# Landmark transposes on both partition halves, and batch 1's loads by halves among the weights, in a fused attention and MLP kernel

## The chip, the cores and the metric

The kernel runs on one core of one Trainium2 chip. The metric is device time in microseconds (us), lower is better. Five engines work on their own instruction queues and meet at semaphores: TensorE (PE in the profile, PEld for its weight loads), VectorE (DVE), ScalarE (ACT), GpSimd (POOL) and SyncE (SP). PE writes to PSUM; DVE and ACT take its results from there into the on-chip memory SBUF. POOL and SP issue transfers to the DMA engines: here POOL issues all loads but the first small one, with a cast from float32 to bfloat16, and SP issues the stores and the transposing transfers.

## The reference

There are 8 batches of 8 heads, 576 tokens and a head width of 64. Each head has 32 landmark rows `p`. The landmarks attend to the tokens, and the tokens then attend to the packed landmarks. The result goes through a two-layer network with a smooth ReLU between (the reference calls its arguments moe, but there is one expert).

```python
def sm_attn(qq, kk, vv):
    s = scale * np.matmul(qq, kk.transpose(0, 1, 3, 2))
    a = np.exp(s - np.max(s, axis=-1, keepdims=True))
    a = a / (np.sum(a, axis=-1, keepdims=True) + 1e-09)
    return np.matmul(a, vv)
p_packed = sm_attn(p, k, v)
x = sm_attn(q, p_packed, p_packed)       # then tokens x 512
h = x @ w_in                             # 512 -> 2048
g = np.where(h >= 1, h, np.where(h <= -1, 0.0, (h + 1) ** 2 / 4))
return g @ w_out                         # 2048 -> 512, 4608 rows
```

## The kernel before

**The work of one batch.** `attention(b, key)` makes these steps, and the letters are the ones that the planner and the profile use. `kT` and `qT`: k and q are transposed by PE for batches 0 to 2 (tile `tp`, L382, copied to SBUF at L325) and by transposing DMAs that SP issues for batches 3 to 7 (L525). Each has two parts of four heads. `sc`: scores of the landmarks (`sp`, L403) and their exponential on ACT (`ex`, L406). `pk`: packed landmarks and their sums (L423, L429), then three small steps on DVE and ACT to `ppT` (L325, L439) and `rs` (L442). `s2`: scores of the tokens (`s`, L457) and `eT` (L462). `sm`: the sums over landmarks (L467), `ln` and `rc` on ACT (L471, L475) and the normalised weights `A` on DVE (L485). `M`: the packed landmarks times one quarter of `w_in` (`mp`, L506), cast to bfloat16 (L325); there are four, `M0` to `M3`, one for each part of `w_in`.

**The network.** `hidden_tile(b, fi)` makes one of 16 tiles of 128 hidden units for the 576 tokens of a batch: four matmuls `h` (L561), one ACT step (L566), one on ACT or DVE (L573 or L571), one DVE step that writes `hT` (L576). `out_tile(pr, i)` makes one of the 9 tiles of 128 output rows of a pair of batches: 16 matmuls `o` of 512 columns (L619), one for each part of `hT`, accumulated in one of two PSUM tiles that are kept for this (`psO`, NO = 2), then a copy to `ob` and the stores by SP (L634). Output tiles 0 to 3 of a pair need batch `2 pr` alone; tiles 4 to 8 need the second batch too.

**Split output tiles.** The parts of `w_out` arrive late at the start. For the first pair, the first `PARTS` output tiles are therefore cut at step `CUT`: the sum up to there is copied out of PSUM to `part` (`kept`, L622), which frees the PSUM tile, and is added when the rest is done (L630). Before, four tiles are cut at step 12, that is, ahead of the last part of `w_out`.

**Landmark transposes.** `add_pT(b0, b1, ...)` (L329) transposes the landmarks of batches b0 to b1 - 1 into `pT`. For each batch one 128x128 transpose on PE (L337) turns two column blocks c (heads 0 to 3, and 4 to 7) at once. `pT` wants head h on the upper or lower 64 partitions according to x, and both are filled, so four copies for (c, x) move 64 partitions each from `tpp` (L343). It is called for batches 0 and 1 at the start, and for batches 2 to 7 after one load `p` (L317) with key 0.9.

**Loads.** The first six are halves of k, v and q of batch 0 (`FIRST`). Then `ORDER` gives the order of the four parts of `w_in` (i0 to i3), the four of `w_out` (o0 to o3), and k, v and q of batch 1; a digit after k, v or q means four of the heads, a bare letter means all eight. Then come `p` and, for each later batch, k, q and v. All go through POOL's one queue, in this order.

**The planner.** Nothing of the order on the chip is decided by the hardware: `Plan.run` places each task on an engine (PE, ACT, DVE, SP, or the DMA queue) at the earliest time by its own clock, using the costs in the table `C`; among tasks that could start at about the same time it prefers the lower key. It writes the instructions of each engine in that order, and at run time each engine keeps to it and waits at semaphores. `C["half"]`, `C["part"]`, `C["w_in"]` and so on are its DMA costs, `C["land"]` the time from the end of a transfer in its model to its landing, `C["xt"]` and `C["xland"]` cost and landing of a transposing DMA. [...] `PB = 2` is the number of batches in the first landmark load. In `psW` there are three large PSUM tiles (NW) for everything but `o`.

Of the kernel before, what the change touches and what calls it, by code (L numbers as in the profile page):

```python
# [8 lines left out]

C = dict(load=3.5666, half=1.46, w_in=2.57, w_out=2.57, rest=1.25, out=9, p=4.05, land=2.0125, xt=6.5, xland=11,
         tpp=0.06, tp=0.042, sc=0.034, pk=0.9765, s2=0.2862, sm=0.245, M=0.2415, h=0.49, o=0.217, switch=0.05,
         join=0.1604, pTc=0.1, Tca=1.12, Tcd=0.76, ex=0.82, ppT=0.42, ppo=0.41, ppa=0.4, ppd=0.2, rs=0.18, eT=0.74,
         ln=0.65, rc=0.68, A=0.82, Mca=1, Mcd=1.22, x=0.65, ta=0.683, td=0.489, hT=0.758, oba=0.585, obd=0.6276,
         array=0.2, wake=1.2, warm=4.2, early=0.3, tell=0.034, feed=0.085, slack=0.51, margin=0.1717, wait=0.5,
         klo=0.05, khi=0.05, part=1.7833)
NW, NO, NX, NB = 3, 2, 5, 6
DW, FILL = 256, 512
PARTS, CUT = 4, 12  # L20

ORDER = "i0 i1 o0 i2 o1 i3 o2 k0 k1 v q0 q1 o3"
TURNED = 3


# [11 lines left out]
class Plan:  # L37
# [152 lines left out]
def kernel(  # L190
# [10 lines left out]
    nc = tc.nc  # L201
    f32 = mybir.dt.float32
    bf16 = mybir.dt.bfloat16
# [18 lines left out]
    X = 2  # L222
# [55 lines left out]
    hT = hid.tile([P, KF, 2 * S], bf16)  # L278
# [5 lines left out]
    L = {}  # L284
# [24 lines left out]
    for nm in ORDER.split():  # L309
# [4 lines left out]
        else:  # L314
            i = int(nm[1])
            L[nm[0], 1, i] = add(DMA, C["part"], -1, (), lambda nm=nm, i=i: load(nm[0], 1, HS[i]))
    L["p"] = add(DMA, C["rest"], -1, (), lambda: nc.gpsimd.dma_start(p_nat[:, PB * 2:], p_v[:, PB * 2:]))  # L317


    def both(fns, cost_a, cost_d, key, deps, **kw):  # L320

        return add((DVE, ACT), {ACT: cost_a, DVE: cost_d}, key, deps, fns, **kw)

    def copy(out_, in_):
        return lambda eng: nc.vector.tensor_copy(out_, in_) if eng == DVE else nc.scalar.copy(out_, in_)  # L325
# [3 lines left out]
    def add_pT(b0, b1, key, deps, cast):  # L329
        n, box = b1 - b0, {}  # L330

        def mm():
            if cast:
                nc.vector.tensor_copy(p_nat[:, 2 * b0:2 * b1], p_raw)
            tp = box["tp"] = wide([P, 8, H // 2, NP], bf16, "tpp")
            for b in range(b0, b1):
                nc.tensor.transpose(tp[:, b - b0].rearrange("p h n -> p (h n)"),  # L337
                                    p_nat[:, 2 * b:2 * b + 2].rearrange("p c d -> p (c d)"), ident)
        t = add(PE, C["tpp"] * n, key, deps, mm, takes="W", readers=4)
        res = []  # L340
# [339 lines left out]
    for b in range(B):  # L680
        if b + 2 < B:
            add_load("k", b + 2, deps=K[b, "kt"])
            add_load("q", b + 2, deps=K[b, "qt"])
            add_load("v", b + 2, deps=K[b, "pk"])
        K[b, "h"] = [hidden_tile(b, fi, b + fi / KF) for fi in range(KF)]
        if b == 0:
            attention(1, keys[1])
            add_pT(PB, B, 0.9, [L["p"]], False)
        if b % 2 == 1:
            for i in range(NT):  # L690
                out_tile(b // 2, i)
        if 0 < b < B - 1:
            attention(b + 1, keys[b + 1])
# [34 lines left out]
```

## Time and profile before

| | us |
|---|---|
| runs of the kernel before: median (lowest to highest of 3) | 248.82 (248.51 to 250.06) |
| the profiled execution: its own time | 249.7 |
| the span in its profile, first to last instruction | 247.8 |
| granted TensorE clock, mean | 1.000 |
| DVE busy | 181.9 (73%), 315 instructions |
| ACT busy | 185.6 (75%), 293 instructions |
| POOL busy | 29.1 (12%), 44 instructions |

All times in the views count from the first instruction of the span. A row of the view of groups gives line, engine, operation, what is written from what, shapes, count, busy time, mean ns of one, and the idle time of the engine just before. In the chain of waits each row has start, duration and what ran. In the table by stretches each engine has its busy time and, in brackets, its instructions; behind them stand the granted clock, the share of the DMA engines in use and the GB/s moved. A DMA row gives the KB and the us from its issue to its landing.

### The profile page before, as it was taken

The page shows a single profiled execution, that of the slowest core. Times are in us where ns is not written, and L with a number is a line of the kernel's source. Part 1 is how long each engine was busy: PE and PEld are TensorE (multiplying, and loading weights), DVE is VectorE, ACT ScalarE, POOL GpSimd, SP SyncE. Part 2 cuts the span into 40 slices and gives each one's busy share as a digit, 9 for nine tenths or more (in the row PEclk, how much of TensorE's full clock was granted, in tenths as well). Part 3 has the DMA queues.
Part 4 walks back from the last instruction along what each step waited for, and adds up shares of the span by engine and source line. Part 5 has one row for each costly group of instructions (what it writes and reads, how often), then busy time and mean ns, then how long its engine had stood idle before and what let it go on. Part 6 is the DMA issues. An engine that isn't in the chain of part 4 may idle for free.

```text
span 247.8 us, 5367 instructions
## 1 busy us (share of the span) xinstructions
PE 235.8 (95%) x2156; PEld 137.5 (55%) x2191; DVE 181.9 (73%) x315; ACT 185.6 (75%) x293; POOL 29.1 (12%) x44
## 2 busy tenths in 40 slices
PE   7979799999989999999999999999999999999994
PEld 2645476367626754666456644665466545654443
DVE  5356988889997988698859884699579976994000
ACT  3259796799899998698769888698888886993110
POOL 8632241211001030011101100000000000000000
PEclk9999999999999999999999999999999999999999
DMA  6999999999999999969796994641662031112222
GB/s 95 194 206 207 206 203 196 202 221 257 169 191 161 218 208 222 209 84 177 158 144 144 170 192 98 131 85 32 115 67 68 7 80 42 46 31 76 64 85 85
DMA packets 54761, 34.37 MB, mean 139 GB/s; under 512 B 27472, under 2 KB 50256, under 8 KB 54736
## 3 DMA queue, kind: packets, MB, share of 16 engines
q0 software_dynamic: 24672, 18.55, 50.3%
q1 hardware_dynamic: 29920, 15.41, 31.4%
q8 instruction: 17, 0.28, 0.5%
q14 instruction: 8, 0.07, 0.1%
q10 hardware_dynamic: 144, 0.07, 0.1%
HBM read 37.22 MB, written 9.44 MB: 188 GB/s over the span
## 4 chain that ended last, share of the span: by engine, by line
PE 76%; DMA 11%; DVE 6%; ACT 3%; issue 2%; POOL 1%; ACTq 0%; POOLq 0%
PE o L619 45%; PE h L561 20%; DMA w_in_sb<-in_moe_w_in_dram 8%; DVE hT L576 3%; DMA k<-in_k_dram 3%; PE mp L506 3%; PE pk L423 2%; PE sp L403 2%; PE tp L382 1%; DVE x L571 1%; PE sm L467 1%; PE s L457 1%; PE pk L429 1%; DVE ob L630 1%; ACT rc L475 1%
## 5 line engine op out<-in xcount | busy, mean ns | idle before, releaser
L619 PE MATMUL o<-w_out_sb,hT 128*128 128x512 bf16 (+2 forms) x559 | 136.0, 373 | 2.4 <-issue 0.8
L576 DVE SCALAR_TENSOR_TENSOR hT<-x 128x576 bf16<-128x576 f32 x128 | 94.6, 755 | 5.1 <-ACT x L573 2.1
L566 ACT ACTIVATE x<-h 128x576 f32<-128x576 f32 x128 | 78.0, 657 | 13.1 <-PE h L561 10.3
L619 PEld LDWEIGHTS <-hT 128*128 128x128 bf16 x592 | 55.2, 98 | 56.3 <-issue 5.8
L561 PE MATMUL h<-A,M 128*128 128x288 bf16 x512 | 75.1, 286 | 1.3 <-ACT M L325 0.5
L561 PEld LDWEIGHTS <-M 128*128 128x128 bf16 x512 | 49.5, 98 | 21.5 <-issue 1.1
L571 DVE TENSOR_SCALAR x<-x 128x576 f32<-128x576 f32 x87 | 39.8, 457 | 11.0 <-ACT x L566 11.0
L573 ACT ACTIVATE x<-x 128x576 f32<-128x576 f32 x41 | 27.2, 682 | 0.1
L325 DVE COPY ob<-o 128x512 f32<-128x512 f32 (+1 forms) x15 | 10.2, 677 | 20.5 <-DMA out_dram<-ob 17.2
L325 ACT COPY ob<-o 128x512 f32<-128x512 f32 (+1 forms) x18 | 10.2, 568 | 19.5 <-PE o L619 19.3
L325 ACT CAST M<-mp 128x1024 bf16<-128x1024 f32 x22 | 21.3, 1019 | 3.7 <-PE mp L506 3.7
L406 ACT ACTIVATE ex<-sp 96x768 bf16<-96x768 f32 x16 | 13.0, 814 | 5.4 <-PE sp L403 5.4
L325 DVE CAST M<-mp 128x1024 bf16<-128x1024 f32 x10 | 12.1, 1220 | 6.2 <-PE mp L506 6.2
L485 DVE SCALAR_TENSOR_TENSOR A<-eT,rs,rc 128x576 bf16<-128x576 bf16 x14 | 11.4, 813 | 5.1 <-ACT rc L475 5.1
L462 ACT ACTIVATE eT<-s,rs 128x576 bf16<-128x576 f32 x16 | 11.3, 739 | 4.7 <-PE s L457 4.7
L268 POOL DMA_DIRECT2D q<-in_q_dram x10 | 7.3, 733 | 49.7 <-DMA qT<-q 34.8
L471 ACT ACTIVATE ln<-sm 128x576 f32<-128x576 f32 x16 | 10.4, 651 | 3.6 <-PE sm L467 3.2
L506 PE MATMUL mp<-w_in_sb,ppT 64*32 64x512 bf16 x256 | 10.5, 380 | 2.6 <-DMA w_in_sb<-in_moe_w_in_dram 2.4
L697 PE MATMUL o<-zeros 128*128 128x512 bf16 (+1 forms) x37 | 11.5, 442 | 1.5 <-DVE zeros L256 1.2
L268 POOL DMA_DIRECT2D k<-in_k_dram x10 | 7.5, 748 | 41.2 <-DMA kT<-k 25.6
L475 ACT ACTIVATE rc<-ln 128x576 f32<-128x576 f32 x16 | 10.9, 683 | 0.5
L403 PEld LDWEIGHTS <-kT 128*128 128x128 bf16 x192 | 7.6, 98 | 2.8 <-DVE kT L325 0.9
(51 smaller groups left out, 120.0 us busy)
## 6 DMA issues: line engine op xcount, KB each, us to landing
out_dram<-ob SPq DMA_DIRECT2D x23, 192.0 KB, 2.3
v<-in_v_dram POOLq DMA_DIRECT2D x7, 576.0 KB, 18.3
k<-in_k_dram POOLq DMA_DIRECT2D x6, 576.0 KB, 12.6
q<-in_q_dram POOLq DMA_DIRECT2D x6, 576.0 KB, 11.8
out_dram<-ob SPq DMA_DIRECT2D x22, 128.0 KB, 3.4
w_in_sb<-in_moe_w_in_dram POOLq DMA_DIRECT2D x4, 512.0 KB, 14.7
w_out_sb<-in_moe_w_out_dram POOLq DMA_DIRECT2D x4, 512.0 KB, 16.8
out_dram<-ob SPq DMA_DIRECT2D x22, 64.0 KB, 2.0
```

The lines of the kernel that those rows point to most:

```text
L268: nc.gpsimd.dma_start(tok[nm, b][:, hs].rearrange("p h c d -> p h (c d)"), SRC[nm][b, hs].rearrange("h (p c) d -> p h (c d)", c=NC))
L325: return lambda eng: nc.vector.tensor_copy(out_, in_) if eng == DVE else nc.scalar.copy(out_, in_)
L403: nc.tensor.matmul(o[:, :, a], kT()[:, i, w:w + P], pT[:, b, h], start=True, stop=True)
L406: nc.scalar.activation(ex()[:, :, i].rearrange("p e x a n -> p e (x a n)"), box["sp"], AF.Exp, scale=scale)
L475: nc.scalar.activation(box["rc"], box["ln"], AF.Exp, scale=-1.0)
L506: nc.tensor.matmul(mp[a * NP:(a + 1) * NP, g], pp_of(y, h), w_in_sb[y * D:(y + 1) * D, h // 2, f * FW:(f + 1) * FW], start=True, stop=True)
L561: nc.tensor.matmul(h[:, hf, :HALF], T[b, "M"][:, g, fi * P:(fi + 1) * P], T[b, "A"][:, g, hf], start=(g == 0), stop=(g == G - 1))
L566: nc.scalar.activation(box["x"], box["h"][:, :, :HALF], AF.Prelu, bias=-1.0, alpha=0.5)
L571: nc.vector.tensor_scalar(x, x, 1.0, 0.0, ALU.add, ALU.max)
L573: nc.scalar.activation(x, x, AF.Relu, bias=1.0)
L576: nc.vector.scalar_tensor_tensor(hT[:, fi, col:col + S].rearrange("p (a t) -> p a t", a=2), box["x"], 1.0, box["x"], ALU.min, ALU.mult)
L619: nc.tensor.matmul(box["o", j][:, :cs.stop - cs.start], hT[:, fi, i * P:(i + 1) * P], w_out_sb[:, fi, cs], start=(fi == 0 or fi in cuts), ...
```

## The change

- `ORDER` is changed from `i0 i1 o0 i2 o1 i3 o2 k0 k1 v q0 q1 o3` to `i0 i1 o0 i2 o1 k0 v0 k1 i3 v1 o2 q1 q0 o3`. Batch 1's v comes in halves, and with it the packing step `pk` of batch 1 is made in two parts of four heads (L538 of the kernel before already chooses so).
- One output tile is cut instead of four, at step 8 instead of 12.
- The landmark transposes write each 64-column block straight to both halves of the partitions: four transposes of 128x64 for a batch instead of one of 128x128, and two copies (for x) of all eight heads instead of four copies of four heads.
- The second landmark load and its transposes are split: batches 2 and 3 (load after o3, key 0.9) and batches 4 to 7 (load after k, q and v of batch 2, key 1.9).
- Many of the planner's costs, the keys of the first attention steps and their order are changed.

```diff
-C = dict(load=3.5666, half=1.46, w_in=2.57, w_out=2.57, rest=1.25, out=9, p=4.05, land=2.0125, xt=6.5, xland=11,
-         tpp=0.06, tp=0.042, sc=0.034, pk=0.9765, s2=0.2862, sm=0.245, M=0.2415, h=0.49, o=0.217, switch=0.05,
...
-         array=0.2, wake=1.2, warm=4.2, early=0.3, tell=0.034, feed=0.085, slack=0.51, margin=0.1717, wait=0.5,
-         klo=0.05, khi=0.05, part=1.7833)
+C = dict(load=3.7557, half=1.46, w_in=2.57, w_out=2.57, rest=1.25, out=5.8085, p=4.05, land=2.9041, xt=4.025,
+         xland=23.0908, tpp=0.06, tp=0.042, sc=0.035, pk=1.0185, s2=0.2115, sm=0.245, M=0.4562, h=0.49, o=0.2105,
...
+         oba=0.5674, obd=0.661, array=0.2, wake=1.2, warm=4.2, early=0.3, tell=0.0394, feed=0.1, slack=0.7935,
+         margin=0.1545, wait=0.465, klo=0.0612, khi=0.0367, part=1.46, p4=1.9)
-PARTS, CUT = 4, 12
+PARTS, CUT = 1, 8
-ORDER = "i0 i1 o0 i2 o1 i3 o2 k0 k1 v q0 q1 o3"
+ORDER = "i0 i1 o0 i2 o1 k0 v0 k1 i3 v1 o2 q1 q0 o3"
-    L["p"] = add(DMA, C["rest"], -1, (), lambda: nc.gpsimd.dma_start(p_nat[:, PB * 2:], p_v[:, PB * 2:]))
+    def add_p(b0, b1):
+        L["p", b0] = add(DMA, C["rest"] * (b1 - b0) / 6, -1, (), lambda: nc.gpsimd.dma_start(p_nat[:, 2 * b0:2 * b1], p_v[:, 2 * b0:2 * b1]))
+    add_p(PB, 4)
-            tp = box["tp"] = wide([P, 8, H // 2, NP], bf16, "tpp")
+            tp = box["tp"] = wide([P, 4, H, NP], bf16, "tpp")
             for b in range(b0, b1):
-                nc.tensor.transpose(tp[:, b - b0].rearrange("p h n -> p (h n)"),
-                                    p_nat[:, 2 * b:2 * b + 2].rearrange("p c d -> p (c d)"), ident)
-        t = add(PE, C["tpp"] * n, key, deps, mm, takes="W", readers=4)
-        for c in range(2):
-            for x in range(X):
-                res.append(both(lambda eng, c=c, x=x: copy(pT[x * D:(x + 1) * D, b0:b1, 4 * c:4 * c + 4, x],
-                                                           box["tp"][c * D:(c + 1) * D, :n])(eng),
-                                C["pTc"] * n, C["pTc"] * n, key, [t], frees=t))
+                for c in range(2):
+                    for x in range(X):
+                        nc.tensor.transpose(tp[x * D:(x + 1) * D, b - b0, 4 * c:4 * c + 4].rearrange("p h n -> p (h n)"),
+                                            p_nat[:, 2 * b + c], ident)
+        t = add(PE, C["tpp"] * n * 2, key, deps, mm, takes="W", readers=X)
+        cost = 0.1 + 0.165 * n
+        res = [both(lambda eng, x=x: copy(pT[x * D:(x + 1) * D, b0:b1, :, x], box["tp"][x * D:(x + 1) * D, :n])(eng),
+                    cost * 1.3, cost, key, [t], frees=t) for x in range(X)]
-    names = "kT0 sc0 pk0 qT0 s20 kT1 sc1 pk1 sm0 qT1 s21 M0 sm1 M1 M2 M3".split()
+    names = "sc0 kT1 pk0 kT0 pk1 sc1 s20 qT0 qT1 M0 s21 sm1 M1 sm0 M2 M3".split()
-    order = "kT0 kT1 sc0 qT0 sc1 qT1 pk0 pk1 s20 M0 s21 sm0 M1 sm1 M2 M3".split()
+    order = "kT0 sc0 kT1 qT0 sc1 qT1 pk0 s20 M0 pk1 sm0 s21 sm1 M1 M2 M3".split()
-            add_pT(PB, B, 0.9, [L["p"]], False)
+            add_pT(PB, 4, 0.9, [L["p", PB]], False)
+            add_p(4, B)
+            add_pT(4, B, C["p4"], [L["p", 4]], False)
```

More of the change, by code (lines that the diff above doesn't have):

```diff
@@ L8 @@
 from concourse._compat import with_exitstack
-C = dict(load=3.5666, half=1.46, w_in=2.57, w_out=2.57, rest=1.25, out=9, p=4.05, land=2.0125, xt=6.5, xland=11,
-         tpp=0.06, tp=0.042, sc=0.034, pk=0.9765, s2=0.2862, sm=0.245, M=0.2415, h=0.49, o=0.217, switch=0.05,
-         join=0.1604, pTc=0.1, Tca=1.12, Tcd=0.76, ex=0.82, ppT=0.42, ppo=0.41, ppa=0.4, ppd=0.2, rs=0.18, eT=0.74,
-         ln=0.65, rc=0.68, A=0.82, Mca=1, Mcd=1.22, x=0.65, ta=0.683, td=0.489, hT=0.758, oba=0.585, obd=0.6276,
-         array=0.2, wake=1.2, warm=4.2, early=0.3, tell=0.034, feed=0.085, slack=0.51, margin=0.1717, wait=0.5,
-         klo=0.05, khi=0.05, part=1.7833)
+C = dict(load=3.7557, half=1.46, w_in=2.57, w_out=2.57, rest=1.25, out=5.8085, p=4.05, land=2.9041, xt=4.025,
+         xland=23.0908, tpp=0.06, tp=0.042, sc=0.035, pk=1.0185, s2=0.2115, sm=0.245, M=0.4562, h=0.49, o=0.2105,
+         switch=0.0658, join=0.1024, pTc=0.1, Tca=1.12, Tcd=0.7372, ex=0.82, ppT=0.42, ppo=0.41, ppa=0.4, ppd=0.2,
+         rs=0.18, eT=0.74, ln=0.65, rc=0.68, A=0.8193, Mca=1, Mcd=1.22, x=0.65, ta=0.683, td=0.457, hT=0.758,
+         oba=0.5674, obd=0.661, array=0.2, wake=1.2, warm=4.2, early=0.3, tell=0.0394, feed=0.1, slack=0.7935,
+         margin=0.1545, wait=0.465, klo=0.0612, khi=0.0367, part=1.46, p4=1.9)
 NW, NO, NX, NB = 3, 2, 5, 6
 DW, FILL = 256, 512
-PARTS, CUT = 4, 12
-ORDER = "i0 i1 o0 i2 o1 i3 o2 k0 k1 v q0 q1 o3"
+PARTS, CUT = 1, 8
+ORDER = "i0 i1 o0 i2 o1 k0 v0 k1 i3 v1 o2 q1 q0 o3"
 TURNED = 3
@@ L334, in mm @@
                 nc.vector.tensor_copy(p_nat[:, 2 * b0:2 * b1], p_raw)
-            tp = box["tp"] = wide([P, 8, H // 2, NP], bf16, "tpp")
+            tp = box["tp"] = wide([P, 4, H, NP], bf16, "tpp")
             for b in range(b0, b1):
-                nc.tensor.transpose(tp[:, b - b0].rearrange("p h n -> p (h n)"),
-                                    p_nat[:, 2 * b:2 * b + 2].rearrange("p c d -> p (c d)"), ident)
-        t = add(PE, C["tpp"] * n, key, deps, mm, takes="W", readers=4)
-        res = []
-        for c in range(2):
-            for x in range(X):
-                res.append(both(lambda eng, c=c, x=x: copy(pT[x * D:(x + 1) * D, b0:b1, 4 * c:4 * c + 4, x],
-                                                           box["tp"][c * D:(c + 1) * D, :n])(eng),
-                                C["pTc"] * n, C["pTc"] * n, key, [t], frees=t))
+                for c in range(2):
[6 more added lines that the diff above has]
+                    cost * 1.3, cost, key, [t], frees=t) for x in range(X)]
         for b in range(b0, b1):
```

## The prediction

> **What bounds the kernel now.** I read the page first (busy shares, the chain's shares), then the table by stretches, then the chain and the timeline around the stretches in which PE is not full.
>
> ```profile
> span 247.8 us, 5367 instructions
> ...
> PE 235.8 (95%) x2156; PEld 137.5 (55%) x2191; DVE 181.9 (73%) x315; ACT 185.6 (75%) x293; POOL 29.1 (12%) x44
> ...
> PE 76%; DMA 11%; DVE 6%; ACT 3%; issue 2%; POOL 1%; ACTq 0%; POOLq 0%
> ```
>
> PE is the bound over the whole span, so the time is PE's work plus what PE loses. DMA's 11% is the start, where loads set the pace. DVE and ACT have 9% together, and it lies in one place, as the stretches show:
>
> ```profile
> 40.00:44.00 4.00, 3.94 (x84) 2.79 (x83) 3.05 (x7) 1.43 (x4) 0.12 (x1) 1.00 1.60 191
> 44.00:48.00 4.00, 3.84 (x53) 1.54 (x47) 3.77 (x5) 3.31 (x5) 1.41 (x2) 1.00 1.35 204
> 48.00:52.00 4.00, 3.47 (x31) 2.11 (x31) 2.71 (x5) 3.83 (x7) 0.00 (x0) 1.00 1.28 224
> 68.00:72.00 4.00, 3.70 (x38) 1.41 (x37) 3.75 (x7) 4.00 (x7) 0.00 (x0) 1.00 1.28 191
> 72.00:76.00 4.00, 3.39 (x37) 1.16 (x36) 3.96 (x7) 3.37 (x6) 0.00 (x0) 1.00 1.28 191
> 88.00:92.00 4.00, 4.00 (x25) 2.15 (x22) 3.32 (x7) 3.98 (x7) 1.50 (x3) 1.00 1.32 176
> ```
>
> The last row is how it goes from 76 us on: PE full. In 40 to 44 ACT works 1.43 of 4 us: batch 0's hidden tiles are done, and batch 1's attention waits for its loads. In 48 to 52 and 68 to 76 PE idles again (0.5, 0.3, 0.6). The chain says for what:
>
> ```profile
> 48.76 0.91 ACT M L325
> 49.71 0.65 PE h L561 x4
> ...
> 73.38 0.39 PE o L619
> ```
>
> Batch 1's first hidden tile starts at 49.71, released by an ACT step. From there to 73.38 the chain runs mostly through DVE and ACT (its 6% and 3% of the page). So two things are for sale before 76 us: when batch 1's hidden tiles start (I call it the gate), and how much work DVE and ACT have after it.
>
> **The change part by part. The loads.** Two single rows each give an issue and its time to landing:
>
> ```profile
> 24.97 0.67 POOL L268 DMA_DIRECT2D q<-in_q_dram  x1 [1.86 <-DMA w_in_sb<-in_moe_w_in_dram]
> 27.55 0.75 POOL L296 DMA_DIRECT2D w_out_sb<-in_moe_w_out_dram  x1 [1.91 <-DMA w_out_sb<-in_moe_w_out_dram]
> ```
> ```profile
> q<-in_q_dram POOLq DMA_DIRECT2D x1, 288.0 KB, 16.2
> ```
> ```profile
> w_out_sb<-in_moe_w_out_dram POOLq DMA_DIRECT2D x1, 512.0 KB, 16.4
> ```
> ```profile
> 11.51 18.82 DMA w_in_sb<-in_moe_w_in_dram
> ```
>
> The last half of q lands at 24.97 + 16.2 = 41.2, o3 at 27.55 + 16.4 = 44.0, i3 at 11.51 + 18.82 = 30.3. The queue moves about 204 GB/s (the row of 44 to 48), so a half of 288 KB takes 1.44 us and a weight part of 512 KB 2.56. The same bytes stand ahead of the last half of q and ahead of o3 in both orders, so both land when they did. Three halves now precede i3: it lands at 30.3 + 4.3 = 34.6, k's first half at about 29.2, v's second at 36.1, o2 at 38.6. The gap that i3's delay opens for batch 0's last four hidden tiles is filled by batch 1's kT, sc and pk, which used to make the thin stretch at 40 to 44. By 38 us the packed landmarks of batch 1 are done, and so M's matmuls and casts no longer compete with the last steps.
>
> **The gate.** After q's last half these steps are in series, and their rows of now are:
>
> ```profile
> 42.90 0.68 PE L382 MATMUL tp<-ident,q 96*128 96x96 bf16 x12
> ...
> 43.62 0.76 DVE L325 COPY qT<-tp 128x1152 bf16<-128x1152 bf16 x1 [0.47 <-PE tp L382]
> ...
> 45.11 0.74 ACT L462 ACTIVATE eT<-s,rs 128x576 bf16<-128x576 f32 x1 [0.48 <-PE s L457]
> ...
> 46.66 0.41 PE L467 MATMUL sm<-eT,onesblk 128*128 128x288 bf16 x2
> ...
> 48.80 0.82 DVE L485 SCALAR_TENSOR_TENSOR A<-eT,rs,rc 128x576 bf16<-128x576 bf16 x1 [0.52 <-ACT rc L475]
> ...
> 49.53 0.68 DVE L325 COPY part<-o 128x512 f32<-128x512 f32 x1
> ```
>
> The transpose starts 1.7 us after the landing, `sm` 0.8 us after `eT` ends (45.85), and 1.7 us lie between `sm`'s end (47.07) and `A`, in which `ln` and `rc` ran on ACT behind those of the other four heads. In series without the first two delays: 0.68 + 0.76 + 0.4 (an estimate for `s` and its hop, 45.11 less the end of the copy at 44.38 being 0.73) + 0.74 + 0.41 + 1.7 + 0.82 = 5.5. From 41.2 that is 46.7 against 49.7: a gain between 0.1 (only the M cast leaves; `A` ends at 49.62 as now) and 3.0. I take 1.9, two thirds, because what stood in front of these steps (pk, both q transposes together, the M casts) is mostly done by then. What is late next is q's landing itself.
>
> **DVE and ACT after the gate.** The landmark copies of now, by size:
>
> ```profile
> L325 DVE COPY pT<-tpp 64x768 bf16<-64x768 bf16 x3 | 1.7, 551 | 0.9 <-ACT pT L325 0.9
> ...
> L325 DVE COPY pT<-tpp 64x256 bf16<-64x256 bf16 x2 | 0.6, 290 | 1.3 <-ACT pT L325 1.3
> ```
>
> Four copies of 768 elements cost at least 4 x 0.55 = 2.2, all on DVE. Between these rows a DVE copy grows by 0.51 ns an element, so one of 512 is 0.42 and one of 1024 is 0.68: two and two make 2.2 as well. The pair for batches 2 and 3 (0.84) may fall ahead of the gate, though. Of the copies of cut tiles three go, and the last of them stands at 49.53 (0.68), behind the gate; the adds become plain copies, which I take to be as long. So 0.7 to 1.5 of work leaves two engines, 0.35 to 0.75 of time; I take 0.6. With the gate, batch 2's hidden tiles start 2.5 us earlier. `pk` of batch 1 in two parts adds some three small DVE or ACT steps ahead of 40 us, in the thin stretch: nothing, as long as it stays thin; about 0.3 otherwise.
>
> **PE's own account.** That gain stays only if PE has done the same work by then:
>
> ```profile
> L619 PEld LDWEIGHTS <-hT x41: 95/98/99, 23.6 to 44.0; 128*128 128x128 bf16 x41
> ```
> ```profile
> L619 PEld LDWEIGHTS <-hT x52: 95/98/99, 23.6 to 48.6; 128*128 128x128 bf16 x52
> ```
> ```profile
> 220.56 10.74 PE o L619 x49
> ```
> ```profile
> L506 PEld LDWEIGHTS <-ppT 64*32 64x32 bf16 x256 | 3.1, 90 | 7.6 <-DMA w_in_sb<-in_moe_w_in_dram 4.0 <-issue 3.0
> ```
>
> By o3's landing 41 `o` steps had been issued, and by the gate 52, at 10.74/49 = 0.219 each in a run. With one cut tile at 8 and two PSUM tiles, at most 8 + 12 + 12 = 32 steps can be done before o3. Between 44.0 and the new gate at 47.8 some 13 more fit beside `s` and `sm`: 45, so 7 are owed (1.5 us). Transposes: 24 for batches 2 to 7 instead of 6. At 128 columns each, a quarter of an `o` step, 0.054, that is 18 x 0.054 = 1.0 more; their loads count 0.1 each if nothing hid them (the nearest rows, 90 ns for a narrow one), 24 x 0.1 - 0.3 = 2.1. I take 1.0. [...]
>
> Against these 2.5 us stands PE's idle time from 44 to 52 and 68 to 76: 0.16 + 0.53 + 0.30 + 0.61 = 1.6, and a lone `o` matmul is booked at 0.39 where it costs 0.219, so some 2.0. Net -0.5.
>
> **Edits at nothing.** The first landmarks: eight small transposes and two copies ahead of 7 us wait for nothing that is late, since k's transposed copy is what the first scores wait for; at worst they add 0.3 to a start that later loads absorb. The load for batches 4 to 7 moves behind k, q and v of batch 2, which land 1.3 us (256 KB) earlier for it; it is needed by scores half a span later. The planner's costs run nowhere on the chip, they change order and the number of filler matmuls: 0, with -0.9 to +0.9. The cost and landing of transposing DMAs move SP's queue and batches 3 to 7's scores, in a region where PE is full and neither kT nor qT releases the chain.
>
> **The sum.** 1.9 + 0.6 - 0.5 = 2.0 us less. The profiled execution (249.7, its span 247.8 and 1.9 around it) would become 247.7. It lies 0.9 above the median of the runs, so on the median's scale 248.8 - 2.0 = 246.8.
>
> **The rivals.** *Larger gain (0.21).* The order falls out as the loads allow: gate 3.0, DVE and ACT 0.75, PE's debt fully hidden in its idle time: 3.75, so 245.1 (244.3 to 245.8). For it speaks that PE's waits for `w_in` (4.0 in the L506 row) may shorten too, since the planner's landing time grows by 0.9 and they show PE ahead of the loads. Against it, that every step of the gate would have to meet an idle engine.
>
> *No change that counts (0.22).* The gate moves by 1 us or less, because A of the second group stays behind other ACT work, or PE's debt is not hidden: 247.8 to 249.5.
>
> *Slower (0.18).* Place: the two PSUM tiles for `o`. From o1's landing on both are held by tiles that cannot end before o3, so PE starves until 44 us. If the planner lets tile 0's rest hold one of them, 24 steps are done instead of 41: 17 x 0.219 = 3.7. If PE finds no idle time later, that and 1.0 of transposes stand against 1.9 + 0.6, or less of those where hidden tiles queue behind `o`: 248.8 + 4.7 - 2.5 = 251.0, to 252.5. It decides where fewer than some 92 steps are done when batch 2's hidden tiles start.
>
> *A start-up cost for each transfer (0.03).* Were a transfer not prepared behind the one before it, the split of v would push q's last half and o3 back. The rows bound this: o3 lands 2.8 after q's last half where its bytes take 2.56, so 0.24 by them, and a half's own time again, 1.44, at the other end. With 1.44 the gate gains 0.5, and the time is 248.2. [...]
>
> **How the numbers follow.** The forecast (gain 1.0 to 3.0, 245.8 to 247.8) has 0.36, and about a third of it lies under 246.3. Runs here tell 1% (2.5 us) from no change. Faster by more: 0.21 + 0.12 = 0.33. Slower by more, above 251.3: most of its rival, 0.14. Within: 0.53. The range from 244.9 to 250.6 leaves out about a tenth on either side.
>
> **What would show it.** Right: first `h` of batch 1 at 47 to 48.5 with q's last half landed at 41 and o3 at 44; ACT in 40 to 44 above 2.5 of 4; fewer than 35 hT loads before 44 but 98 or more by batch 2's first `h`, at 73 to 75; PE idle under 1 us in the four stretches from 44 to 52 and 68 to 76. Wrong: the gate at 49 or later; q landing after 42.5; transposes above 0.08 each; PE idle between 30 and 44 above 4 us; or a new wait behind 76 us, where I expect the rest to be shifted as it is.

## The result, and the profile after

| | before | after |
|---|---|---|
| median of the runs, us (lowest to highest of 20 each) | 249.38 (248.51 to 250.06) | 249.69 (249.25 to 250.32) |
| the profiled execution, us | 249.7 | 249.65 |
| its span, us | 247.8 | 247.6 |

The ratio is 1.0016, with a 95% interval of 1.0008 to 1.0023: the change costs 0.3 us by the medians (0.2 to 0.6 by the interval), where a gain of 2.0 was forecast. The median of before over 20 runs lies 0.56 above that of the three runs that the forecast started from, so its 246.8 would stand at 247.4 on this scale. The single profiled executions differ by 0.05 in their own time and by 0.2 in their spans, the other way, so the views below can place microseconds, not the last half of one. Some executions got a granted clock of 0.991 to 0.993 and took one to four us longer; five of the twelve runs of e2 and four of the twelve of e9 below are of this kind, and their other runs have medians of 249.59 and 249.28, within 0.15 of before's in the same rounds.

The page of the kernel after, span, engines and the chain's shares by engine:

```profile
span 247.6 us, 5464 instructions
...
PE 239.8 (97%) x2217; PEld 138.6 (56%) x2217; DVE 184.6 (75%) x312; ACT 185.0 (75%) x295; POOL 30.4 (12%) x46
...
PE 81%; DMA 10%; DVE 3%; ACT 3%; issue 1%; POOL 1%; ACTq 0%; POOLq 0%
```

DVE and ACT hold 6% of the chain now instead of 9%, and PE's share of busy time grew from 95 to 97%. One caution for reading this: the page of before has 2156 matmul records for 2191 weight loads, that of after 2217 for both. Some matmuls of before are missing from its trace, so part of its "idle" PE time is only missing records. The 0.16 us at 45.20 is of this kind (two weight loads stand there for one matmul); the two longest waits that the prediction counted, 0.47 ahead of 49.71 and 0.56 ahead of 73.38, are not, since there every load has its matmul. Counts of weight loads are the safe measure, and I use them for the account.

The table by stretches of after, columns as before (us, then PE, PEld, DVE, ACT, POOL, each with its instructions, clock, DMA share, GB/s):

```profile
40.00:44.00 4.00, 3.76 (x73) 1.85 (x71) 3.87 (x6) 3.50 (x5) 1.75 (x3) 1.00 1.38 197
...
44.00:48.00 4.00, 4.00 (x35) 2.06 (x34) 3.92 (x7) 3.72 (x6) 0.56 (x1) 1.00 1.32 204
48.00:52.00 4.00, 4.00 (x51) 2.81 (x47) 2.83 (x6) 3.16 (x6) 0.77 (x1) 1.00 1.42 199
...
68.00:72.00 4.00, 4.00 (x41) 1.71 (x40) 3.11 (x5) 2.59 (x5) 0.00 (x0) 1.00 1.28 191
72.00:76.00 4.00, 4.00 (x42) 1.73 (x40) 3.07 (x5) 3.53 (x7) 0.00 (x0) 1.00 1.38 166
```

ACT's thin stretch from 40 to 44 is filled (3.50 instead of 1.43), and PE is full in the four stretches in which it had idled by 0.16, 0.53, 0.30 and 0.61. Yet the time did not fall. The reason is in two places: when batch 1's first hidden tile starts, and how many `o` steps PE has done by then. The loads of batch 1 came as forecast. Single rows of after, q's last half and o3, with issue and time to landing:

```profile
27.12 0.67 POOL L268 DMA_DIRECT2D q<-in_q_dram  x1 [1.91 <-DMA w_out_sb<-in_moe_w_out_dram]
28.89 0.75 POOL L296 DMA_DIRECT2D w_out_sb<-in_moe_w_out_dram  x1 [1.09 <-DMA k<-in_k_dram]
```
```profile
q<-in_q_dram POOLq DMA_DIRECT2D x1, 288.0 KB, 13.9
```
```profile
w_out_sb<-in_moe_w_out_dram POOLq DMA_DIRECT2D x1, 512.0 KB, 14.6
```

They land at 27.12 + 13.9 = 41.0 and 28.89 + 14.6 = 43.5, forecast 41.2 and 44.0. PE does not starve while the loads come: it works 13.43 of the 14 us from 30 to 44 (13.46 before). What follows the landing is the surprise. The timeline of after, all engines together, from the landing to the first hidden tile of batch 1 (L564 is `h`, L328 the copies, L465 `eT`, L470 `sm`, L474 `ln`, L478 `rc`, L488 `A`, L622 `o`):

```profile
41.41 0.67 PE L385 MATMUL tp<-ident,q 96*128 96x96 bf16 x12 [0.24 <-DVE qT L328]
...
42.12 0.76 DVE L328 COPY qT<-tp 128x1152 bf16<-128x1152 bf16 x1
...
42.52 0.76 ACT L465 ACTIVATE eT<-s,rs 128x576 bf16<-128x576 f32 x1
...
43.23 0.31 PE L460 MATMUL s<-qT,ppT 64*32 64x288 bf16 x8
...
43.62 0.74 ACT L465 ACTIVATE eT<-s,rs 128x576 bf16<-128x576 f32 x1 [0.34 <-PE s L460]
...
43.69 1.47 PE L622 MATMUL o<-w_out_sb,hT 128*128 128x512 bf16 x6
...
44.25 1.00 ACT L328 CAST M<-mp 128x1024 bf16<-128x1024 f32 x1
...
44.99 0.80 PE L470 MATMUL sm<-eT,onesblk 128*128 128x288 bf16 x4
...
45.44 0.65 ACT L474 ACTIVATE ln<-sm 128x576 f32<-128x576 f32 x1 [0.18 <-PE sm L470]
...
46.12 0.69 ACT L478 ACTIVATE rc<-ln 128x576 f32<-128x576 f32 x1
...
46.84 0.65 ACT L474 ACTIVATE ln<-sm 128x576 f32<-128x576 f32 x1
...
47.52 0.68 ACT L478 ACTIVATE rc<-ln 128x576 f32<-128x576 f32 x1
47.59 1.19 PE L385 MATMUL tp<-ident,k 96*128 96x96 bf16 x24
48.14 0.69 DVE L328 COPY ob<-o 128x512 f32<-128x512 f32 x1
...
48.61 1.51 PE L622 MATMUL o<-w_out_sb,hT 128*128 128x512 bf16 x6
48.75 0.81 DVE L488 SCALAR_TENSOR_TENSOR A<-eT,rs,rc 128x576 bf16<-128x576 bf16 x1
...
49.96 0.41 PE L564 MATMUL h<-A,M 128*128 128x288 bf16 x2
```

Batch 1's first `h` is at 49.96, and it was at 49.71 before. The transposes start 0.4 us after the landing. The score matmul of the second group starts 0.35 after its copy ends. `sm` starts at 44.99, 0.63 us after `eT` ends, and in PE's queue six `o` matmuls stand ahead of it. Both groups' sums are made together, although the first group's `eT` had ended at 43.28. The four steps `ln`, `rc`, `ln`, `rc` then run in series on ACT, from 45.44 to 48.20. `A` comes 0.55 after the last of them, behind a copy of an output tile on DVE, and `h` 0.4 after `A`, behind six more `o`. No engine was short of work; each held something else in its queue just ahead of the step that mattered.

The same series stood on ACT before, and it was as long, 2.76 us from 46.00 to 48.76. Before's first `sm`, its first `ln` and its last `rc`:

```profile
45.56 0.40 PE L467 MATMUL sm<-eT,onesblk 128*128 128x288 bf16 x2
...
46.00 0.65 ACT L471 ACTIVATE ln<-sm 128x576 f32<-128x576 f32 x1
...
48.08 0.68 ACT L475 ACTIVATE rc<-ln 128x576 f32<-128x576 f32 x1
```

So the change brought this series forward by 0.56 us only, and the output copy on DVE and the `o` matmuls ahead of `h` took that back.

How much PE did by when, in weight loads of `o` with an `hT` part (after, each up to the end of a window: 44, the first `h` of batch 1, the first `h` of batch 2):

```profile
L622 PEld LDWEIGHTS <-hT x29: 95/98/99, 23.6 to 43.9; 128*128 128x128 bf16 x29
```
```profile
L622 PEld LDWEIGHTS <-hT x45: 95/98/99, 23.6 to 49.5; 128*128 128x128 bf16 x45
```
```profile
L622 PEld LDWEIGHTS <-hT x109: 95/98/99, 23.6 to 77.0; 128*128 128x128 bf16 x109
```

And before, up to the first `h` of batch 2, which starts there at 76.45 and in after at 77.38:

```profile
L619 PEld LDWEIGHTS <-hT x104: 95/98/99, 23.6 to 76.0; 128*128 128x128 bf16 x104
```
```profile
77.38 0.41 PE L564 MATMUL h<-A,M 128*128 128x288 bf16 x2
```
```profile
76.45 1.39 PE L561 MATMUL h<-A,M 128*128 128x288 bf16 x10
```

The account, at the prediction's 0.219 us a step. **To the gate:** 45 steps instead of 52, so 7 x 0.219 = 1.5 behind, and 0.25 later. **From the gate to batch 2's first `h`:** 64 steps in 77.38 - 49.96 = 27.42 us, before 52 steps in 76.45 - 49.71 = 26.74; 12 steps more (2.6) in 0.68 more: 1.95 won back. In after the 24 transposes of batch 2's k (1.19 in the timeline) stand ahead of the gate, and before they stood behind it (50.63 and 52.71), so some 1.2 of the 1.95 is work that changed sides. The rest, about 0.75, is idle time that is gone, less the 16 landmark transposes at 64.54, which stand behind the gate only in after. **Together:** 1.95 - 1.5 - 0.25 = 0.2 us ahead in the profiled executions. After 77 us nothing new happens: 247.6 - 77.38 = 170.2 us against 171.35, and the five steps that after has in hand (109 against 104) are 1.1 of it.

### The profile page after: what moved, and what is told of

The parts are those of the page before. It is cut to its first block, busy times and chain, and to the rows that moved or that the text cites. A ratio compares the mean times of both kernels' runs of the same rounds, so it can differ in the third digit from the quotient of the medians.

```text
span 247.6 us, 5464 instructions
## 1 busy us (share of the span) xinstructions
PE 239.8 (97%) x2217; PEld 138.6 (56%) x2217; DVE 184.6 (75%) x312; ACT 185.0 (75%) x295; POOL 30.4 (12%) x46
## 4 chain that ended last, share of the span: by engine, by line
PE 81%; DMA 10%; DVE 3%; ACT 3%; issue 1%; POOL 1%; ACTq 0%; POOLq 0%
PE o L622 49%; PE h L564 22%; DMA k<-in_k_dram 10%; PE mp L509 3%; PE sp L406 2%; PE sm L470 1%; PE pk L426 1%; ACT x L569 1%; DVE hT L579 1%; PE tp L385 1%; PE s L460 1%; DVE x L574 1%; PE pk L432 1%; ACT qT L328 0%; ACT M L328 0%
## 5 line engine op out<-in xcount | busy, mean ns | idle before, releaser
L622 PE MATMUL o<-w_out_sb,hT 128*128 128x512 bf16 (+2 forms) x592 | 143.7, 374 | 0.0
L622 PEld LDWEIGHTS <-hT 128*128 128x128 bf16 x592 | 55.0, 98 | 55.2 <-issue 5.3
L564 PE MATMUL h<-A,M 128*128 128x288 bf16 x512 | 75.8, 286 | 0.2
L564 PEld LDWEIGHTS <-M 128*128 128x128 bf16 x512 | 49.4, 98 | 22.2 <-issue 0.7
L574 DVE TENSOR_SCALAR x<-x 128x576 f32<-128x576 f32 x77 | 35.1, 455 | 13.7 <-ACT x L569 13.6
L576 ACT ACTIVATE x<-x 128x576 f32<-128x576 f32 x51 | 33.9, 681 | 0.2
L328 DVE COPY ob<-o 128x512 f32<-128x512 f32 (+1 forms) x18 | 12.3, 683 | 20.7 <-PE o L622 20.4
L328 ACT COPY ob<-o 128x512 f32<-128x512 f32 (+1 forms) x18 | 10.2, 566 | 23.2 <-PE o L622 23.2
L328 DVE CAST M<-mp 128x1024 bf16<-128x1024 f32 x16 | 19.4, 1222 | 4.2 <-PE mp L509 3.8
L328 ACT CAST M<-mp 128x1024 bf16<-128x1024 f32 x16 | 15.7, 1013 | 2.5 <-PE mp L509 2.3
L488 DVE SCALAR_TENSOR_TENSOR A<-eT,rs,rc 128x576 bf16<-128x576 bf16 x14 | 11.4, 815 | 4.5 <-ACT rc L478 4.4
L465 ACT ACTIVATE eT<-s,rs 128x576 bf16<-128x576 f32 x16 | 11.3, 737 | 4.6 <-PE s L460 4.6
L702 PE MATMUL o<-zeros 128*128 128x512 bf16 (+1 forms) x41 | 12.3, 430 | 1.2 <-DVE zeros L256 1.2
L474 ACT ACTIVATE ln<-sm 128x576 f32<-128x576 f32 x16 | 10.4, 650 | 3.5 <-PE sm L470 3.3
L478 ACT ACTIVATE rc<-ln 128x576 f32<-128x576 f32 x16 | 10.9, 683 | 0.5
L268 POOL DMA_DIRECT2D v<-in_v_dram x10 | 7.3, 730 | 32.3 <-PE pk L426 14.9
## 6 DMA issues: line engine op xcount, KB each, us to landing
k<-in_k_dram POOLq DMA_DIRECT2D x6, 576.0 KB, 13.9
```

The lines of the kernel that those rows point to most:

```text
L268: nc.gpsimd.dma_start(tok[nm, b][:, hs].rearrange("p h c d -> p h (c d)"), SRC[nm][b, hs].rearrange("h (p c) d -> p h (c d)", c=NC))
L488: nc.vector.scalar_tensor_tensor(A()[:, g], box["eT"], rs()[:, g, :1], box["rc"], ALU.mult, ALU.mult)
L564: nc.tensor.matmul(h[:, hf, :HALF], T[b, "M"][:, g, fi * P:(fi + 1) * P], T[b, "A"][:, g, hf], start=(g == 0), stop=(g == G - 1))
L574: nc.vector.tensor_scalar(x, x, 1.0, 0.0, ALU.add, ALU.max)
L576: nc.scalar.activation(x, x, AF.Relu, bias=1.0)
L622: nc.tensor.matmul(box["o", j][:, :cs.stop - cs.start], hT[:, fi, i * P:(i + 1) * P], w_out_sb[:, fi, cs], start=(fi == 0 or fi in cuts), ...
```

## The experiments

Each ratio is to the kernel before, with its 95% interval, and after stood at 1.0016 (1.0008 to 1.0023). "Against after" is the difference of two such ratios times 249.4 us. Two kinds have to be kept apart: edits inside a planned step, which leave the written order of all other instructions alone, and edits that change what the planner reads, which order everything anew. The labels e1 to e15 are those by which the expectations name the runs.

**The transposes, doubled (e1).** Each landmark transpose of after is issued twice, order kept:

```diff
-                for c in range(2):
+                for c in (0, 0, 1, 1):
```

> The kernel after with each landmark transpose issued twice into the same place; the order on every engine is otherwise the same. Theory A (from 44 us on PE is full in the kernel after, so the time is PE's work plus what PE loses before 44 us): 24 of the 32 extra transposes lie behind 44 us at 0.053 each, 1.3 us slower than the kernel after. Theory B (the first hidden tile of batch 1 and the work of DVE and ACT set the pace to 76 us): the extra transposes fit into PE's gaps, 0 to 0.3 slower. Theory C (narrow transposes cost more than their columns): 2.4 us or more.

Measured 250.43 us, ratio 1.0040 (1.0023 to 1.0057): 0.6 more than after. The rows of the timeline for the group of batches 4 to 7 give the price of one. First after, then this kernel, then the next experiment's, which turns 128 columns at once, and at last before's group of six:

```profile
64.54 0.64 PE L342 MATMUL tpp<-ident,p_nat 128*64 128x128 bf16 x16
```
```profile
65.08 1.08 PE L342 MATMUL tpp<-ident,p_nat 128*64 128x128 bf16 x32
```
```profile
64.74 0.61 PE L342 MATMUL tpp<-ident,p_nat 128*128 128x128 bf16 x8
```
```profile
48.10 0.49 PE L337 MATMUL tpp<-ident,p_nat 128*128 128x128 bf16 x6
```

Sixteen more narrow transposes take 0.44 us, 0.0275 each, half of the 0.054 that I had counted. Two more wide ones take 0.61 - 0.49 = 0.12, 0.06 each. The 24 extra ones behind the start are 0.65 us of PE, and the kernel lost 0.6 (0.1 to 1.1 by the intervals): that fits the full price, the interval is too wide to show it, and the price is small. Theory C's 2.4 is excluded.

**One transpose for two (e2).** Landmarks are stored twice side by side in after, so that one 128-column transpose fills both partition halves, order kept (its loads are issued twice):

```diff
...
-                    for x in range(X):
-                        nc.tensor.transpose(tp[x * D:(x + 1) * D, b - b0, 4 * c:4 * c + 4].rearrange("p h n -> p (h n)"),
-                                            p_nat[:, 2 * b + c], ident)
+                    nc.tensor.transpose(tp[:, b - b0, 4 * c:4 * c + 4].rearrange("p h n -> p (h n)"),
+                                        p_nat[:, 2 * b + c].rearrange("p u d -> p (u d)"), ident)
```

> The kernel after with the landmarks stored twice side by side, so that one 128-column transpose fills both halves of the partitions: 16 transposes in place of 32, 12 fewer behind 44 us, and each landmark load issued twice. Theory A: 0.6 us faster than the kernel after. Theory B: no change. Theory C: 1.2 us faster or more. If the doubled loads delay k, q and v of batch 2, up to 0.5 slower.

Measured 249.93 us, ratio 1.0033 (1.0009 to 1.0057): not told apart from after, and Theory A's 0.6 faster did not come. By the rows, eight wide ones in 0.61 and sixteen narrow ones in 0.64 are nearly the same work, so halving their number had next to nothing to sell.

**The old landmarks in the new kernel (e3, e9).** After with before's transposes and four copies, planned anew:

```diff
-                for c in range(2):
-                    for x in range(X):
...
+                nc.tensor.transpose(tp[:, b - b0].rearrange("p h n -> p (h n)"),
+                                    p_nat[:, 2 * b:2 * b + 2].rearrange("p c d -> p (c d)"), ident)
+        t = add(PE, C["tpp"] * n, key, deps, mm, takes="W", readers=4)
...
```

> The kernel after with the transposes and the four copies of the kernel before, the two later landmark loads kept apart. Theory A: 18 transposes fewer behind 44 us, 1.0 us faster than the kernel after, although DVE and ACT get up to 0.7 us more work. Theory B: 0 to 0.5 slower.

Measured 251.21 us, ratio 1.0072 (1.0052 to 1.0092): 1.4 slower than after, which no theory had. Either the old copies are that dear, or the new plan is a worse order. Later, the same wide transposes and four copies were put inside after's planned steps, so that the order stays (e9):

```diff
...
-        res = [both(lambda eng, x=x: copy(pT[x * D:(x + 1) * D, b0:b1, :, x], box["tp"][x * D:(x + 1) * D, :n])(eng),
+        res = [both(lambda eng, x=x: [copy(pT[x * D:(x + 1) * D, b0:b1, 4 * c:4 * c + 4, x], box["tp"][c * D:(c + 1) * D, :n])(eng) for c in (x, 1 - x)],
```

> The kernel after with the wide transposes and four copies of the kernel before, issued inside the same planned steps, so that the order on all engines stays that of the kernel after. PE has 18 transposes fewer behind 44 us (0.96 us), DVE and ACT some 0.6 more together. By the prices that the runs e5 to e8 gave (in the kernel after a us of PE costs 0.9, one of DVE 0.7): about 0.5 faster than the kernel after (0 to 0.9). Theory G (the order that the planner writes makes the difference in e3): not slower, although e3 was 1.4 slower with the same instructions in another order. Rival H (the four copies themselves are slow, for their place or their waits): 0.8 to 1.5 slower.

Measured 249.53 us, ratio 1.0025 (1.0003 to 1.0048): not told apart from after, and by the ratios 1.2 us (0.4 to 1.9) faster than the same landmarks planned anew. So most of the loss of the first try was its order.

**Four cut tiles (e4).** After with four output tiles cut at step 8, to pay PE's debt ahead of o3; this too is planned anew:

```diff
-PARTS, CUT = 1, 8
+PARTS, CUT = 4, 8
```

> The kernel after with four output tiles cut at step 8 instead of one. Theory A: more output steps can be done before the last part of w_out lands (29 before 44 us in the kernel after, 41 in the kernel before), PE loses 1.0 to 1.5 us less before 44 us, and the time is 1.0 to 1.5 us less than the kernel after. Theory B: three more copies on DVE or ACT, 0.5 to 1.0 slower.

Measured 251.75 us, ratio 1.0089 (1.0073 to 1.0104): 1.8 slower than after. The weight loads of `o` up to 44 us and the last hidden tile of batch 0 in its trace:

```profile
L622 PEld LDWEIGHTS <-hT x29: 95/98/99, 24.3 to 43.9; 128*128 128x128 bf16 x29
```
```profile
47.57 0.65 PE L564 MATMUL h<-A,M 128*128 128x288 bf16 x4
...
49.48 1.20 PE L564 MATMUL h<-A,M 128*128 128x288 bf16 x8 [0.74 <-ACT M L328]
```

The planner did not use the freedom: still 29 steps by 44, and batch 0's last hidden tile came at 47.57, 9 us later than in after, where it is among the eight matmuls from 38.09. The last row is batch 1's first hidden tile: it starts 0.5 us earlier than in after, and yet the time is 1.8 longer, so the gate alone does not set the time. Whether four cuts would pay in an order that uses them stays open.

**What a microsecond of an engine costs (e5 to e8).** One more `h` matmul in each of batch 1's 16 hidden tiles (16 x 0.12 = 1.9 us of PE, since four take 0.49 in before's chain of waits, at 140.40), order kept, in before (e5) and in after (e7):

```diff
+            if b == 1:
+                nc.tensor.matmul(h[:, 0, :HALF], T[b, "M"][:, 0, fi * P:(fi + 1) * P], T[b, "A"][:, 0, 0], start=True, stop=True)
```

> The kernel before with one h matmul of 288 columns more (0.12 us, written over by the next) in each of the 16 hidden tiles of batch 1: 1.9 us of PE work between 49 and 67 us, the order otherwise the same. Theory D (only PE's lost time can be saved; in the kernel before PE loses 4.5 us between 44 and 80 us, in the kernel after 1.7): most of it is hidden, 0 to 0.7 us slower than the kernel before. Rival E (PE is the bound in both): 1.9 slower.

> The kernel after with the same 16 additional h matmuls, 1.9 us of PE work. Theory D: PE is full from 44 us on, so 1.4 to 1.9 us slower than the kernel after. Rival F (PE's full rows hide slack as in the kernel before, and DVE and ACT still set the pace): 0 to 0.7.

Measured in before 250.59 us, ratio 1.0054 (1.0040 to 1.0068): 1.35 us, 0.7 for each us of PE, between Theory D's and Rival E's. In after 251.42 us, 1.0086 (1.0073 to 1.0100): 1.75 against after, 0.9 for each, as Theory D says.

The same with DVE (e6 in before, e8 in after): 64 columns of `hT` are written a second time in each of those tiles.

```diff
+            if b == 1:
+                nc.vector.scalar_tensor_tensor(hT[:, fi, col:col + 64], box["x"][:, 0, :64], 1.0, box["x"][:, 0, :64], ALU.min, ALU.mult)
```

> The kernel before with a short second step on DVE (64 of the 576 columns of hT written again) in each hidden tile of batch 1, an estimated 2.3 us of DVE work between 50 and 73 us. Theory D: DVE sets the pace there and PE has nothing else to do, so 1.2 to 2.3 us slower than the kernel before. Rival E: 0 to 0.5.

> The kernel after with the same 16 additional DVE steps, an estimated 2.3 us. Theory D: PE has output steps to go on with, so 0 to 0.7 us slower than the kernel after. Rival F: 1.2 to 2.3.

The groups of the two kernels, before's first:

```profile
L579 DVE SCALAR_TENSOR_TENSOR hT<-x 128x64 bf16<-128x64 f32 x16 | 3.6, 225 | 0.6
```
```profile
L582 DVE SCALAR_TENSOR_TENSOR hT<-x 128x64 bf16<-128x64 f32 x16 | 3.6, 225 | 0.6
```

Measured in before 252.82 us, ratio 1.0147 (1.0130 to 1.0164): 3.7 us for 3.6 of DVE, the whole price. In after 252.1 us, 1.0117 (1.0103 to 1.0131): 2.5 against after, 0.7 for each us. I had expected DVE to be nearly free in after; it isn't. DVE became cheaper, 1.0 to 0.7, and the difference of 1.1 us is clear of the noise; that PE became dearer, 0.7 to 0.9, is within it (0.4 us, give or take 0.5). DVE's price goes with its load in this place: between batch 1's first hidden tile and batch 2's it works 24.77 of 26.74 us before (93%) and 23.51 of 27.42 in after (86%), where its share of the whole span is 73 and 75%. So the change made some slack on DVE here, and sold none of it; ACT's price was not tried.

**The order alone (e11, e12).** One of the planner's costs, which nothing on the chip reads, is set 12 ns higher, in after and in before:

```diff
-... hT=0.758 ...
+... hT=0.77 ...
```

> The kernel after with one cost of the planner changed by 12 ns (hT 0.758 to 0.770): the same work in a somewhat different order. Theory G: the time moves by 0.5 to 2 us, most likely up. Rival I (orders from nearly the same costs are worth the same): within 0.3 of the kernel after.

> The same change of one planner cost in the kernel before. Theory G: 0.5 to 2 us, most likely up. Rival I: within 0.3 of the kernel before.

Measured for after 252.31 us, ratio 1.0119 (1.0103 to 1.0135), 2.6 us slower than after; for before 252.36 us, 1.0125 (1.0108 to 1.0142), 3.1 us slower than before. Both are more than Theory G's 0.5 to 2. Stretches of the two, after's and then before's:

```profile
76.00:80.00 4.00, 3.31 (x21) 1.91 (x21) 3.93 (x6) 2.70 (x5) 0.45 (x1) 1.00 1.21 171
```
```profile
32.00:36.00 4.00, 3.12 (x28) 1.83 (x28) 3.31 (x5) 2.61 (x4) 1.55 (x2) 1.00 1.31 203
```

PE loses 0.7 us in a place where it had been full, and 0.9 in another where it had lost 0.05. Batch 1's first hidden tile starts at 51.70 and 51.14 in these two, 1.7 and 1.4 later than in after and before. In both cases a new order from nearly the same costs was 1.0 to 1.25% slower, more than any part of the change that could be measured. So the two kernels that were planned anew (old landmarks in e3, four cut tiles) say little about their edits.

**The gate: work or order? (e13, e14)** If DVE and ACT were too busy ahead of the gate, taking work from them there must bring it forward. The second elementwise step of batch 0's last four hidden tiles is left out, 2.1 us of DVE and ACT together, order kept:

```diff
+            if b == 0 and fi >= 12:
+                return
```

> The kernel after without the second elementwise step of the last four hidden tiles of batch 0 (1.4 us of DVE and 0.7 of ACT between 39 and 46 us are left out, so those outputs lack a step); the order otherwise the same. Theory J (the late third part of w_in has moved these tiles into the steps that lead to batch 1's first hidden tile, and they hold it up): that tile starts 0.4 us or more earlier than at 49.8, and by the price of DVE in e8 the time is 0.5 to 1.2 us less than the kernel after. Rival K (q's landing and PE's queue alone set that start): 0 to 0.3.

> The same step left out in the kernel before, where these tiles run at 35 to 40 us, ahead of the stretch in which ACT works 1.43 of 4 us. Theory J: the thin stretch takes it up and the start of batch 1's first hidden tile stays, 0 to 0.3 less than the kernel before. Rival K: the same as e13.

Measured for after 249.65 us, ratio 1.0015 (1.0000 to 1.0030), for before 249.12 us, 0.9994 (0.9981 to 1.0006): no gain in either. The timeline of the first, at the gate (the line of `o` is two lower there, L624):

```profile
43.98 1.47 PE L624 MATMUL o<-w_out_sb,hT 128*128 128x512 bf16 x6
...
45.28 0.65 PE L470 MATMUL sm<-eT,onesblk 128*128 128x288 bf16 x4
...
50.05 1.14 PE L564 MATMUL h<-A,M 128*128 128x288 bf16 x8
```

`sm` still stands behind the `o` matmuls and `h` still starts at 50. So it isn't the amount of this work that holds the gate, and Theory J is out. That the place in the queues holds it is read from the timeline; no run moved one of these steps in its queue.

**The landmarks alone, in before's order (e10).** Narrow transposes and two copies inside before's planned steps:

```diff
-                nc.tensor.transpose(tp[:, b - b0].rearrange("p h n -> p (h n)"),
-                                    p_nat[:, 2 * b:2 * b + 2].rearrange("p c d -> p (c d)"), ident)
+                for c in range(2):
+                    for x in range(X):
+                        nc.tensor.transpose(tp[x * D:(x + 1) * D, b - b0, 4 * c:4 * c + 4].rearrange("p h n -> p (h n)"),
+                                            p_nat[:, 2 * b + c], ident)
...
+                res.append(both(lambda eng, c=c, x=x: c or copy(pT[x * D:(x + 1) * D, b0:b1, :, x], box["tp"][x * D:(x + 1) * D, :n])(eng),
```

> The kernel before with the narrow transposes and two copies of the kernel after, for the same batches and in the same planned steps: 18 transposes more behind 44 us, copies 0.5 us shorter. By the prices of e5 and e6 (PE 0.7, DVE 1.0): 0.2 slower than the kernel before (0 to 0.6). Rival H: 0.5 to 1.0 faster.

Measured 248.71 us, ratio 0.9980 (0.9969 to 0.9990): 0.5 us faster than before and 0.9 faster than after, the best version of the study. The group of its copies for batches 2 to 7, and its first `h` of batch 1 in the chain of waits:

```profile
L325 DVE COPY pT<-tpp 64x1536 bf16<-64x1536 bf16 x2 | 1.9, 950 | 0.0
```
```profile
49.14 0.65 PE h L562 x4
```

Two copies in 1.9 us stand for four in 2.45 (three of 551 ns on DVE, and in before's trace one of 795 on ACT), and the gate is at 49.14 instead of 49.71. I had expected 0.2 slower, with 0.96 us for the transposes; with the 0.3 that they measure (24 x 0.0275 less 6 x 0.06) and the prices of e5 and e6, 0.2 slower for PE and 0.55 faster for the copies make 0.35 faster, which the interval allows.

The same with the landmarks stored twice and one wide transpose for two (e15):

```diff
-    p_nat = const.tile([P, B * 2, D], bf16)
+    p_nat = const.tile([P, B * 2, 2, D], bf16)
...
```

> The kernel of e10 (the kernel before, its order, two copies) with the landmarks stored twice, so that one wide transpose fills both halves: 12 transposes fewer behind 44 us (0.64 us of PE) against e10, and the landmark load of batches 2 to 7 issued twice (some 1.0 us later landings of k, q and v of batch 2, which have 2 us or more in hand). By the price of PE in e5: 0.4 faster than e10, 0.9 faster than the kernel before. If the loads delay batch 2: no gain on e10.

Measured 248.78 us, ratio 0.9985 (0.9973 to 0.9997): faster than before, and not told apart from the narrow form, as in after. The 0.4 expected against the narrow form rested on 0.64 us of transposes, which the rows above don't bear out.

## Why the prediction was wrong

**The step that failed is the gate term, 1.9 us.** The first hidden tile of batch 1 was put at 47.8 and came at 49.96, 0.25 later than before. The landing that the term counted from was right (41.0). So were the durations in series: the rows after have the same 0.67, 0.76, 0.74 and 0.81. What failed is the reason for taking two thirds of the possible gain: that what stood in front of these steps would be done by then. The work named there left only in part: batch 1's packed landmarks were done at 39.4 and not by 38, M's matmuls from 43.01 stand ahead of the second group's `s`, and the last M casts start at 44.12 and 44.25 (one pair started at 48.67 before). Other work was put there: `o` matmuls ahead of `sm` and `h` and an output copy ahead of `A`. And the series of four ACT steps, which the sum counted only from the second group's `sm` on (the 1.7), starts with the first group's sums, and these were issued with the second group's, at 44.99, where the first `eT` had ended at 43.28.

What the bare chain of 5.5 us lacked can be added up from the timeline: 0.4 ahead of the transposes, 0.35 ahead of `s`, 0.63 ahead of `sm`, 0.4 ahead of `h`, and from the start of `sm` to the start of `A` 48.75 - 44.99 = 3.76 where 0.41 + 1.7 were assumed, 1.65 more (0.55 of it behind the output copy). That makes 3.4, and 41.0 + 5.5 + 3.4 = 49.9; the forecast of 47.8 had left room for 1.1 of it. That the gate holds without 2.1 us of elementwise work on DVE and ACT shows that this work isn't the cause. Which of these waits weighs most was not tried one by one, and that moving the steps in their queues would bring the gate forward is not shown.

**PE's account came near in sum, in part by luck.** The debt at the gate is the 7 steps (1.5 us) forecast, but they were forecast for a gate at 47.8. At 47.8 after had issued 39 steps, and it came to 45 because its gate was 2.2 us later. Behind the gate the other terms, 0.6 + 2.0 - 1.0 = 1.6, stand against 1.95 measured, of which 1.2 is k's transposes, which no term had. The terms also count some time twice. Of PE's idle time, 0.16 + 0.47 lies ahead of 49.71, and an earlier gate contains it already; 0.16 and 0.56 of the rest are waits for DVE, which the 0.6 of DVE and ACT had sold. By the prediction's own first step the time is PE's work plus what PE loses, so each such wait can be saved once. As the terms were put, 1.9 - 1.5 + 1.6 = 2.0 was forecast and -0.25 - 1.5 + 1.95 = 0.2 came in the profiled execution; the runs put it at -0.3.

**The transposes** were taken as 1.0 and measure 24 x 0.0275 less 6 x 0.06, 0.3. The bound of 2.1 is not borne out: 16 narrow transposes with their loads take 0.64 us, 8 wide ones 0.61.

**The copies** were right in size. Two of 512 and two of 1024 elements were put at 0.42 and 0.68, and DVE's take 0.417 and 0.695:

```profile
L328 DVE COPY pT<-tpp 64x512 bf16<-64x512 bf16 x3 | 1.3, 417 | 0.7 <-PE tpp L342 0.7
...
L328 DVE COPY pT<-tpp 64x1024 bf16<-64x1024 bf16 x1 | 0.7, 695 | 0.0
```

Between batch 1's first hidden tile and batch 2's, DVE and ACT together do 49.98 us of work before and 47.80 in after, so 2.2 left them where 0.7 to 1.5 was counted. Counting half of DVE's or ACT's time, since two engines share it, was too low as well: a us of DVE costs 0.7 to 1.0 by the runs. So this term was not what was lacking.

**The rivals.** "No change that counts" named this case, with its first mechanism (A of the second group stays behind other ACT work, and for the last 0.55 us behind a copy on DVE) and not its second. The larger gain needed an idle engine at each step of the gate, and the gate moved the other way. The slower rival's place was real, with 29 steps by 44, but its deciding point was not reached: 109 steps were done by batch 2's first `h`, where it needed fewer than 92. A start-up cost for each transfer is excluded here by the landings at 41.0 and 43.5, no later than the 41.2 and 44.0 of the forecast. Batch 2's first `h` was expected at 73 to 75 and came at 77.38: the gate is 2.2 of it, and 109 `o` steps were done ahead of it where the forecast asked for 98.

**What is settled.** The landmark part alone gains 0.5 us in before's order, and in after's it can't be told from nothing. So the rest of the change (the order of loads, the split landmark load, the cut, costs and keys) costs 0.9 us (0.6 to 1.2) against the best version. Its parts can't be priced singly by these runs, since each of them makes the planner write a new order, and a new order alone moved the time by 1%.

## What to carry to other kernels

Where the order of each engine is written out ahead of time, work that is done earlier, as batch 1's k and v here, need not bring the next step forward: follow the chain from the last landing and ask at each step what is queued ahead of it. Where one engine is the bound, count a saving once, as time that this engine no longer loses; an earlier start and the wait ahead of it are the same microseconds. Test an edit inside the written order, unchanged, before letting a planner write a new one, and measure what a new order alone does (here 12 ns in one cost made 2.6 to 3.1 us). Compare two traces by instructions done up to the same point, weight loads where matmul records may be missing, not by idle time.

## What the runs showed of the hardware

Two 64-column transposes that go to opposite halves of the partitions cost no more here than one of 128 columns: 0.0275 us each (16 more of them took 0.44 in e1), against 0.06 for a wide one (eight took 0.61 in e2, six 0.49 in before). And a busy share of 73 to 75% over the span did not mean slack in one stretch of it: 3.6 us of DVE spread over one batch's hidden tiles, where DVE was 93% busy before and 86% after, cost 3.7 and 2.5 us of the whole, in kernels in which PE is the bound.
